# A scheduled attention and MoE kernel: weight signs by ScalarE, scales from squares, one unit fewer in float32

## The chip, the cores and the metric

The kernel runs on one core of a Trainium2 chip. The metric is the device time of one execution in microseconds, less being better. A core has TensorE (PE in the profile; its weight loads are PEld), VectorE (DVE), ScalarE (ACT), GpSimd (POOL), SyncE (SP, which only issues DMAs here) and sixteen DMA engines. Matrix products are written to PSUM, everything else lies in SBUF.

## The reference

```python
# attention with a feature map; q, k, v are (8, 8, 576, 64) float32, w_phi (64, 128)
def phi(x):
    proj = np.einsum('bhsd,df->bhsf', x, w_phi)
    proj = proj - np.max(np.abs(proj), axis=-1, keepdims=True)
    return np.concatenate([np.exp(proj), np.exp(-proj)], axis=-1)
q_p, k_p = phi(q), phi(k)
kv = np.einsum('bhsf,bhsd->bhfd', k_p, v)
z = np.sum(k_p, axis=2)
num = np.einsum('bhsf,bhfd->bhsd', q_p, kv)
den = np.einsum('bhsf,bhf->bhs', q_p, z)[..., None] + 1e-06
attn = (num / den).astype(np.float32)
# then one dense feed-forward; x is (4608, 512), w_in (512, 2048), w_out (2048, 512)
x = attn.transpose(0, 2, 1, 3).reshape(4608, 512)
h = x @ w_in
g = h * (1.0 / (1.0 + np.exp(-1.702 * h)))
out = (g @ w_out).astype(np.float32)
```

`w_in` and `w_out` arrive as float64 and reach the kernel as 64-bit integers.

## The kernel before, in words

**Attention.** The work is cut into 32 units. Unit `i = 4*b + hp` is batch `b` and head pair `hp`: keys and queries of two heads, 512 of the 576 rows. The other 64 rows of all eight heads of a batch (the tail) are handled once a batch by `attn_tail`. A unit can run in two ways. Exact units (`i < NEX`, six of them) work in whole float32: `project_whole` transposes the rows on TensorE and multiplies by `wb`, and each float32 product costs two passes. Split units write each float32 number as a high and a low 16-bit part: `project` makes the two parts on ScalarE and VectorE, turns them by a transposing DMA, and multiplies by `ph`; `features_k` and `features_q` take exponentials, and `parts` forms high parts (`eh`, ScalarE) and low parts (`el`, VectorE's subtraction). The tail always has such parts. In batch 0 its high and low parts are both of the 4-byte type `F32R`, in the other batches the low parts are 16-bit.

**Weights.** There are 32 blocks of 128 x 512 (16 of `w_in`, 16 of `w_out`), prepared in two halves (`NH = 2`). `load_weights` reads a block of float64 into `raw`, views it as a low and a high 32-bit word, and puts a float32 together: POOL scales the high word so that its exponent fits, ScalarE converts the low word, and VectorE merges them, with the sign set last, in two instructions:

```python
R.vector.scalar_tensor_tensor(z, y.bitcast(I32), 3, z, ALU.logical_shift_left, ALU.bitwise_or)
R.vector.scalar_tensor_tensor(
    dst.bitcast(I32), hi, -(2**31), z, ALU.bitwise_and, ALU.bitwise_or)
```

Then four matmuls per block with a one-hot stationary block of nine columns, `pick`, add up the magnitudes by columns in PSUM (`wsum`). `weight_scales` turns those sums into one power-of-two scale for each of the two matrices, and `split_weights` writes each block as a high and a low float16 part, in place.

**MoE.** `moe_chunk` handles 256 or 384 rows at a time over sixteen slices `j` of the hidden width: for each it makes `hb` (three matmuls per 128 of the width: high by high, high by low, low by high), the activation (`th`, `g`), its parts `gh` and `gl`, and three products into each accumulator `ab`. The first 512 rows run half by half, so that they can start when the first half of the weights is ready. The last chunk's three accumulators go to `osb`, `osb` and `e` by ScalarE, and SP stores them, each in two pieces.

**The order of the work.** Nothing is issued as written. Every instruction goes through a `Recorder`, which notes what it reads and writes and its price (`cost`). `R.part(v0, v1)` gives the following instructions virtual times, on a scale where 1 is one MoE chunk of 384 rows and 0 the start of the MoE. `v_att` gives those of the attention units, `V1` those of batch 1, `WV` those of the weights. `schedule` then plays all five engines: each takes, of the instructions whose operands its price list says are ready, the one with the lowest virtual time. Buffers (`NB`, the number of each kind) are handed out in the same play. The result is a fixed order per engine; at run time an engine waits on semaphores for what its next instruction needs and passes nothing by. All instructions therefore bear one line number in the profile, that of the call in `emit`, and are told apart by the names of their tiles.

Of the kernel before, what the change touches and what calls it, by code (L numbers as in the profile page):

```python
# [8 lines left out]
F32 = mybir.dt.float32  # L9
# [3 lines left out]
I32 = mybir.dt.int32  # L13
U32 = mybir.dt.uint32
# [75 lines left out]
class _Op:  # L90
    __slots__ = (
        "eng", "meth", "args", "kw", "cost", "deps", "left", "outs", "allocs", "uses",
        "prio", "load", "passes", "end", "est", "also", "start",
    )


_READY = {"tensor": 282.5, "scalar": 240.0, "vector": 305.0, "gpsimd": 300.0, "sync": 100.0}
# [13 lines left out]
class Recorder:  # L111
# [12 lines left out]

    def tile(self, buf, whole=False):
        tl = _Tile(buf, whole)
        return V(tl, (), buf.aps[0])


    def record(self, eng, meth, args, kw, also):  # L130
        o = _Op()
        o.eng, o.meth, o.args, o.kw = eng, meth, args, kw
# [59 lines left out]
    def cost(eng, meth, args, kw):  # L192
# [9 lines left out]
        if eng == "tensor":  # L202

            wide = mybir.dt.size(ap[1].dtype) == 4
            load = ap[1].shape[-1] / (1.2 if wide else 4.6)
            if meth == "transpose":
# [4 lines left out]
            return (load, n / 2.4 + (14.0 if wide else 3.0), 1)  # L211
# [23 lines left out]


    def schedule(self):
# [16 lines left out]
        pipe, turn, port = 0.0, 0.0, 0.0  # L254
# [20 lines left out]
        while todo:  # L275
            best = None
            for e, c in cand.items():
                t = free[e]
                pick = None
                for o in c:  # L280
                    s = max(t, o.est, turn + o.load) if e == "tensor" else max(t, o.est)
                    ok = True
                    for tl in o.allocs:
                        b = tl.buf
                        if b.ordered and b.head != tl.turn:
                            ok = False
                            break
                        av = [a for a, w in zip(b.avail, b.owner) if w is None]
                        if not av:
                            ok = False  # L290
                            break
                        s = max(s, min(av) + 175.0) if b.head >= len(b.aps) else s
# [26 lines left out]
            elif o.eng == "tensor":  # L319
                turn = s  # L320
# [20 lines left out]
    def emit(self):  # L341
        g = lambda a: a.get() if isinstance(a, V) else a
        self.order = self.schedule()
        for o in self.order:
            f = getattr(getattr(self.nc, o.eng), o.meth)
            f(*[g(a) for a in o.args], **{k: g(a) for k, a in o.kw.items()})  # L346
# [3 lines left out]
def attn_moe_kernel(ctx, tc, q, k, v, w_phi, w_in, w_out, out):  # L350
# [11 lines left out]
    NEX = 6  # L362
# [12 lines left out]
    def static(name, shape, dt):  # L375
# [6 lines left out]
        kq=2, vn=1, xs=2, xT=2, ks=12, tl=1, t=4, e=2, eh=3, el=2, ekth=1, ektl=1,  # L382
        eqth=1, eqtl=1, xf=1, kzs=1, kf=1, lq=2, nf=1, nt=1, xo=1, x=3, th=2, g=2, gh=2,
# [5 lines left out]
        e=([P, 1024], F32), eh=([P, 512], F32R), el=([P, 512], F32R),  # L389
        ekth=([P, 512], F32R), ektl=([P, 512], F32R),  # L390
        eqth=([P, 512], F32R), eqtl=([P, 512], F32R),
# [11 lines left out]
    for nm in ("eh", "el", "ekth", "ektl", "eqth", "eqtl"):  # L403
        pools[nm + "6"] = buf(nm + "6", [P, 512], F16, NB[nm])
    for nm in ("el", "ektl", "eqtl"):
        pools[nm + "b"] = buf(nm + "b", [P, 512], BF16, NB[nm])
# [20 lines left out]
    ones = cp.tile([16, P], F32, name="ones")  # L427
    nc.gpsimd.memset(ones, 1.0)

# [39 lines left out]

    NS = NJ // NH + 1  # L470
    pick = cp.tile([P, 2 * NS - 1], BF16, name="pick")
    nc.gpsimd.memset(pick, 0.0)
    nc.gpsimd.memset(pick[:, NS - 1 : NS], 1.0)

    def load_weights(j, wsum, first, last):
# [4 lines left out]
        for i, src in (  # L480
# [4 lines left out]
            if not WIDE:  # L485
# [3 lines left out]
                z = new("osb")  # L489
                R.scalar.activation(z, wbuf[:, i + 1], AF.Abs)  # L490
            else:
# [3 lines left out]
                else:  # L495
# [165 lines left out]
    pools["kzb"] = buf("kzb", [P, 2, DV], BF16, 1)  # L661
# [12 lines left out]
    for ap in (f32(vs0), v60, f32(vt0), vt60):  # L674
# [6 lines left out]
    for a in range(2):  # L681
        r = slice(a * D, a * D + D)
        for ap in (f32(vt0), vt60):
            nc.gpsimd.memset(ap[r, :, a, 0, D : D + 1], 1.0)

# [121 lines left out]
    def attn_tail(b, tl, exact, bank):  # L807
# [9 lines left out]
        if b == 0:  # L817
            for a in range(2):
# [5 lines left out]
            return ekt, eqt, (vt, vt)  # L824
# [422 lines left out]
```

## Time and profile before

| | |
|---|---|
| median of 3 runs | 1099.08 us (1098.79 to 1100.6) |
| the profiled execution | 1097.82 us |
| its span, first to last instruction | 1096.0 us |
| TensorE busy | 1062.2 us (97%) |
| VectorE busy | 857.8 us (78%) |
| ScalarE busy | 712.2 us (65%) |
| POOL busy | 242.4 us (22%) |
| moved by DMA | 87.80 MB |

How to read the profile's lines. A group line has engine, operation, output and inputs by the program's names (buffer numbers left out), partitions x elements and type, count, busy time in us, the mean duration of one in ns, and the idle time of the engine just before them with what ended it. For matmuls two more sizes stand ahead, rows * columns of the stationary block. A timeline line has start and length in us, then the same, for a run of like instructions (x count), and in brackets the wait before it. A line of stages has the stretch, its length, busy us and count of PE, PEld, DVE, ACT and POOL, the granted clock, the DMA engines' share and GB/s. Matmuls overlap, so that a matmul's duration is longer than what it adds to a run, and busy time of TensorE isn't all work.

### The profile page before, as it was taken

What the parts mean: (1) busy time and instruction counts of PE and PEld (TensorE: products, weight loads), DVE (VectorE), ACT (ScalarE), POOL (GpSimd) and SP (SyncE); (2) the same over time, 40 slices, a digit from 0 to 9 for tenths busy, and PEclk for the clock granted to TensorE, in tenths of its full rate; (3) what the DMA queues carried; (4) which work ended last, traced back from release to release, by engine and by line L of the source; (5) the groups of instructions that cost most, each with busy time, mean ns of one, the idle gap of its engine ahead of it and who ended that gap; (6) DMA issues with size and microseconds to landing.
All of it is one profiled execution on the core that took longest, in us unless ns stands there. A gap on an engine that the chain in (4) does not pass through costs nothing.

```text
span 1096.0 us, 22834 instructions
## 1 busy us (share of the span) xinstructions
PE 1062.2 (97%) x8915; PEld 733.2 (67%) x8915; DVE 857.8 (78%) x1775; ACT 712.2 (65%) x1483; POOL 242.4 (22%) x310
## 2 busy tenths in 40 slices
PE   5997999999999999999999999999999999999997
PEld 3664677778766666678766666677876666577653
DVE  5889988999989997897789987897779877422322
ACT  4576687977677776676777677685677666432423
POOL 6546201322121212221132221121123111100000
PEclk9998999999999999999999999999999999999999
DMA  8854233454243431442243433333223220000101
GB/s 273 277 185 130 76 92 84 79 107 98 61 93 92 96 89 36 81 107 57 32 102 88 109 88 55 64 97 60 49 68 68 39 59 10 11 30 1 30 1 29
DMA packets 174252, 87.80 MB, mean 80 GB/s; under 512 B 140224, under 2 KB 164928, under 8 KB 173888
## 3 DMA queue, kind: packets, MB, share of 16 engines
q1 hardware_dynamic: 174144, 86.34, 33.0%
q8 instruction: 70, 1.15, 0.5%
q14 instruction: 38, 0.31, 0.1%
HBM read 54.59 MB, written 9.44 MB: 58 GB/s over the span
## 4 chain that ended last, share of the span: by engine, by line
PE 78%; DVE 10%; ACT 4%; issue 3%; DMA 2%; POOL 1%; SPq 1%; ACTq 0%; DVEq 0%; POOLq 0%
PE ab L346 31%; PE hb L346 29%; PE at L346 19%; DMA xT<-xs 1%; DVE sm L346 1%; DVE gl L346 1%; ACT e L346 1%; DVE ks L346 1%; DVE g L346 1%; DVE t L346 1%; ACT eh L346 1%; SPq L346 1%; DVE el L346 1%; DVE elb L346 1%; DMA tl<-in_v_dram 1%
## 5 line engine op out<-in xcount | busy, mean ns | idle before, releaser
L346 PE MATMUL hb<-x,wbuf 128*128 128x192 f16 (+3 forms) x3264 | 474.9, 280 | 1.1 <-DVE g L346 1.1
L346 PE MATMUL ab<-wbuf,gh 128*128 128x512 f16 x1152 | 335.8, 380 | 0.8 <-ACT gh L346 0.6
L346 PEld LDWEIGHTS <-wbuf 128*128 128x128 f16 x3264 | 279.1, 98 | 78.0 <-issue 0.9
L346 ACT ACTIVATE th<-hb,usc 128x384 f32<-128x384 f32 (+1 forms) x208 | 116.4, 560 | 130.7 <-PE hb L346 125.0
L346 PE MATMUL ab<-wbuf,gl 128*128 128x512 f16 x576 | 192.2, 380 | 1.3 <-DVE gl L346 1.1
L346 DVE SCALAR_TENSOR_TENSOR g<-th,hb 128x384 f32<-128x384 f32 (+1 forms) x208 | 107.6, 517 | 89.8 <-ACT th L346 87.5
L346 PEld LDWEIGHTS <-gh 128*128 128x128 f16 x1152 | 107.3, 98 | 80.4 <-ACT gh L346 2.9
L346 ACT ACTIVATE gh<-g,al 128x384 f16<-128x384 f32 (+1 forms) x176 | 107.6, 611 | 62.7 <-DVE g L346 62.4
L346 DVE SCALAR_TENSOR_TENSOR gl<-g,al,gh 128x384 f16<-128x384 f32 (+1 forms) x176 | 110.9, 630 | 39.2 <-ACT gh L346 32.9
L346 POOL TENSOR_TENSOR xf<-nf,rc 128x512 f32<-128x512 f32 x28 | 32.8, 1171 | 459.4 <-DVE rc L346 395.1
L346 PE MATMUL at<-ph,xT 128*128 128x128 f16 x944 | 108.6, 221 | 0.4 <-ACT x L346 0.4
L346 ACT ACTIVATE e<-at 128x512 f32<-128x512 f32 x144 | 85.6, 602 | 30.3 <-PE at L346 28.5
L346 DVE TENSOR_REDUCE sm<-at 128x4 f32<-128x512 f32 x126 | 86.1, 683 | 21.3 <-PE at L346 21.1
L346 ACT ACTIVATE e<-t 128x512 f32<-128x512 f32 x144 | 89.9, 640 | 9.8 <-DVE t L346 8.6
L346 PEld LDWEIGHTS <-gl 128*128 128x128 f16 x576 | 55.1, 98 | 51.1 <-DVE gl L346 7.2
L346 DVE SCALAR_TENSOR_TENSOR t<-at,ks,sm 128x512 f32<-128x512 f32 x118 | 87.5, 744 | 1.0
L346 DVE TENSOR_TENSOR el<-e,eh 128x512 f16<-128x512 f32 (+1 forms) x106 | 74.7, 704 | 12.7 <-ACT eh L346 11.1
L346 PE MATMUL at<-vs,eh 128*128 128x132 f32 x208 | 80.2, 386 | 0.0
L346 DVE TENSOR_TENSOR elb<-e,eh 128x512 bf16<-128x512 f32 x104 | 74.8, 719 | 6.7 <-ACT eh L346 6.5
L346 PEld LDWEIGHTS <-xT 128*128 128x128 f16 x944 | 70.2, 98 | 14.3 <-issue 1.3
L346 PE MATMUL at<-kzs,eh 128*128 128x132 f32 x216 | 78.2, 375 | 0.0
L346 ACT ACTIVATE eh<-t 128x512 fp32r<-128x512 f32 x105 | 66.4, 648 | 0.3 <-DVE t L346 0.2
(205 smaller groups left out, 1896.4 us busy)
## 6 DMA issues: line engine op xcount, KB each, us to landing
vn<-in_v_dram SPq DMA_DIRECT2D x64, 128.0 KB, 2.9
kq<-in_k_dram SPq DMA_DIRECT2D x32, 256.0 KB, 3.2
kq<-in_q_dram SPq DMA_DIRECT2D x32, 256.0 KB, 3.0
tl<-in_v_dram SPq DMA_DIRECT2D x18, 384.0 KB, 3.2
x<-in_moe_w_in_dram SPq DMA_DIRECT2D x10, 512.0 KB, 5.3
x<-in_moe_w_out_dram SPq DMA_DIRECT2D x10, 512.0 KB, 4.8
out_dram<-osb SPq DMA_DIRECT2D x38, 128.0 KB, 2.4
out_dram<-osb SPq DMA_DIRECT2D x16, 256.0 KB, 2.5
```

Of the source, the lines that this page charges most:

```text
L346: f(*[g(a) for a in o.args], **{k: g(a) for k, a in o.kw.items()})
```

## The change

1. The sign of a weight is no longer set by VectorE. After the low word's conversion, ScalarE multiplies the high word by a tiny number with a float16 output: what is left is a 16-bit zero that keeps the sign, written into the upper half of the converted low word. One VectorE instruction then merges everything.
2. The scale of a matrix no longer comes from sums of magnitudes. For each 128 columns of a block TensorE multiplies the upper 16 bits (bfloat16) of the finished float32 weights by themselves, so that the diagonal of the 128 x 128 result sums squares; `weight_scales` takes the maximum, transposes, takes it again, halves the exponent by a shift and hands out both scales by one matmul. `pick` is gone.
3. `NEX` is 5 instead of 6: unit 5 becomes a split unit.
4. In batch 0 the low parts are bfloat16, with 16-bit copies of the tail's values (`vtb`) and of `kf` (`kzb`), both written by POOL. In `two`, all `el` kinds now end in `b`.
5. Buffers: `t` 5 instead of 4, `e` 3 instead of 2; the `F32R` low parts are gone.
6. The last chunk: its first accumulator still goes out by ScalarE, the second and third by VectorE, and the second one's stores are issued by ScalarE's queue instead of SP's.
7. The play of the order: a change of stationary size costs TensorE 95 ns, a 4-byte stationary block 22 ns instead of 14, small 16-bit stationary blocks at least 105; several ordered buffers can be taken by one instruction. A new method `pairs` isn't called.
8. Virtual times: as in the diff.

```diff
-    NEX = 6
+    NEX = 5
...
-        kq=2, vn=1, xs=2, xT=2, ks=12, tl=1, t=4, e=2, eh=3, el=2, ekth=1, ektl=1,
-        eqth=1, eqtl=1, xf=1, kzs=1, kf=1, lq=2, nf=1, nt=1, xo=1, x=3, th=2, g=2, gh=2,
+        kq=2, vn=1, xs=2, xT=2, ks=12, tl=1, t=5, e=3, eh=3, ekth=1, eqth=1, xf=1, kzs=1, kf=1, lq=2, nf=1, nt=1, xo=1, x=3, th=2, g=2, gh=2,
...
                 y = wbuf[:, i + 1]
+                R.scalar.activation(lo, lo.bitcast(U32), AF.Copy, scale=0.9375 * 2.0**-29)
                 R.gpsimd.tensor_scalar(y, hi.bitcast(F32), 2.0**-112, None, ALU.mult)
-                z = lo
-                R.scalar.activation(z, lo.bitcast(U32), AF.Copy, scale=0.9375 * 2.0**-29)
+
+                sign = raw.bitcast(F16).rearrange("p (n w) -> p n w", w=4)[:, :, 1]
+                R.scalar.activation(sign, hi.bitcast(F32), AF.Copy, scale=2.0**-60)
                 R.vector.scalar_tensor_tensor(
-                    z, y.bitcast(I32), 3, z, ALU.logical_shift_left, ALU.bitwise_or
+                    y.bitcast(I32), y.bitcast(I32), 3, lo, ALU.logical_shift_left, ALU.bitwise_or
                 )
-                R.vector.scalar_tensor_tensor(
-                    dst.bitcast(I32), hi, -(2**31), z, ALU.bitwise_and, ALU.bitwise_or
-                )
-                z = raw.bitcast(BF16).rearrange("p (n w) -> p n w", w=4)[:, :, 1]
-
-            r = NS - 1 if i % 2 else j % (NS - 1)
+            z = wbuf[:, i + 1].bitcast(BF16).rearrange("p (n w) -> p n w", w=2)[:, :, 1]
             for c in range(NCT):
+                zc = z[:, c * P : (c + 1) * P]
                 R.tensor.matmul(
-                    wsum,
-                    pick[:, NS - 1 - r : 2 * NS - 1 - r],
-                    z[:, c * P : (c + 1) * P],
+                    wsq[:, i % 2],
+                    zc,
+                    zc,
...
-    def weight_scales(k, wsum):
+    def weight_scales(k, wsq):
-        m = small(1, "sc")[0:NS]
-        m2 = small(NS, "sc")[0:NS]
-        R.vector.tensor_reduce(m, wsum, AX.X, ALU.max)
-        pow2(m, m)
-        R.vector.tensor_scalar(m2, ident[0:NS, 0:NS], m, None, ALU.mult)
+        m = small(2, "sc")
+        m1 = small(1, "sc")[0:2]
+        m2 = small(2, "sc")[0:2]
+        R.vector.tensor_reduce(m, wsq, AX.X, ALU.max)
         tp = psa()
-        R.tensor.matmul(tp[:, 0:NS], ones[0:NS], m2, start=True, stop=True)
-        R.vector.tensor_reduce(wg[:, k, 0:1], tp[:, 0 : NS - 1], AX.X, ALU.max)
-        R.vector.tensor_copy(wg[:, k, 1:2], tp[:, NS - 1 : NS])
+        R.tensor.transpose(tp[0:2, 0:P], m, ident)
+        R.vector.tensor_reduce(m1, tp[0:2, 0:P], AX.X, ALU.max)
+        R.vector.tensor_scalar(
+            m1.bitcast(I32), m1.bitcast(I32), 1, 0x7F800000,
+            ALU.logical_shift_right, ALU.bitwise_and,
+        )
+        R.vector.tensor_scalar(m1, m1, 2.0**64, 2.0**-50, ALU.mult, ALU.max)
+        R.vector.tensor_scalar(m2, wone, m1, None, ALU.mult)
+        R.tensor.matmul(tp[:, P : P + 2], ones[0:2], m2, start=True, stop=True)
+        R.vector.tensor_copy(wg[:, k], tp[:, P : P + 2])
...
-        if b:
-            return new(nm + "6"), new(nm + "b" if spare == "el" else nm)
-        return new(spare), new(nm)
+        w = "b" if spare == "el" else ""
+        return new(nm + "6") if b else new(spare + w), new(nm + w)
...
+                R.gpsimd.tensor_copy(vtb[r, :, a, 0:D], tl[r, 2])
-            return ekt, eqt, (vt, vt)
+            return ekt, eqt, (vt, vt, vtb)
...
-            kzl = [z[:, :, 0] for z in kz]
+            kzl = new("kzb")
+            R.gpsimd.tensor_copy(kzl, kf)
+            kzl = [kzl[:, s] for s in range(2)]
...
+            end = c0 + n == SB * S and sb == B // SB - 1
+            osb = new("e")[:, 0:DM] if end and m == n // P - 1 else new("osb")
...
+            elif end and m:
+                R.vector.tensor_scalar(osb, acc[m], osc[:, sb : sb + 1], None, ALU.mult)
+            else:
+                R.scalar.activation(osb, acc[m], AF.Copy, scale=osc[:, sb : sb + 1])
+            store(sb, c0 + m * P, osb, R.scalar if end and m == 1 else R.sync)
...
-    V1 = (-1.1375, 0.5)
-    WV = ((-9.8, 0.3, -7.2), (-7.1, 0.2, -5.4))
+    V1 = (-1.506, 0.476)
+    WV = ((-9.335, 0.3, -7.2), (-7.049, 0.2, -5.399))
+    SV = ((-0.438, 0.02), (0.0, 0.227))
     def v_att(i):
         if i < 4:
-            return -10.175 + i
+            return -10.175 + 0.987 * i
         if i < 8:
             return V1[0] + (i - 4) * V1[1]
-        return 0.825 + (i - 8) * 0.3625
+        return 0.825 + (i - 8) * 0.348
...
-                R.part(u, u + (0.27 if b else 0.1))
+                R.part(u, u + (0.176 if b else 0.1))
...
-            R.part(w, w + (0.54 if b else 0.2))
+            R.part(w, w + (0.537 if b else 0.2))
...
-        R.part(v1, v1 + 0.1, ("vector", "scalar"))
+        v2 = v1 + SV[part_][0]
+        R.part(v2, v2 + SV[part_][1], ("vector", "scalar"))
         for j in js:
             split_weights(j)
```

More of the change, by code (lines that the diff above doesn't have):

```diff
@@ L92 @@
         "eng", "meth", "args", "kw", "cost", "deps", "left", "outs", "allocs", "uses",
-        "prio", "load", "passes", "end", "est", "also", "start",
+        "prio", "load", "passes", "end", "est", "also", "start", "calls",
     )
+_SWITCH = 0.0
 _READY = {"tensor": 282.5, "scalar": 240.0, "vector": 305.0, "gpsimd": 300.0, "sync": 100.0}
@@ L123, in part, with pairs @@
         self.first = first
+    def pairs(self, mm, also=()):
+        o = _Op()
+        o.eng, o.meth, o.args, o.kw, o.calls = "tensor", "matmul", (), {}, mm
+        c = [self.cost("tensor", "matmul", a, k) for a, k in mm]
+        o.load, o.cost, o.passes = c[0][0], _SWITCH + sum(x[1] * x[2] for x in c) / 2, 1
+        o.deps, o.outs, o.allocs, o.uses = {}, [], [], []
+        o.end, o.est = None, 0.0
+        for a, _ in mm:
+            for i in (1, 2):
+                if isinstance(a[i], V):
+                    self.touch(o, a[i], False)
+        for a, _ in mm:
+            self.touch(o, a[0], True)
+        for a in also:
+            self.claim(o, a.tl)
+        o.left = len(o.deps)
+        for d in o.deps:
+            d.outs.append(o)
+        self.group.append(o)
+        o.prio = o.eng in self.first
+        self.ops.append(o)
     def tile(self, buf, whole=False):
@@ L205, in cost @@
             load = ap[1].shape[-1] / (1.2 if wide else 4.6)
+            if ap[1].shape[-1] <= 64 and not wide:
+                return (105.0, max(105.0, n / 2.4), 1)
             if meth == "transpose":
@@ L234, in cost, with mode @@
         return 400.0
+    @staticmethod
+    def mode(o, i):
+        if o.calls:
+            return o.calls
+        st = o.args[1].t if isinstance(o.args[1], V) else o.args[1]
+        n = st.shape[-1] if i else st.shape[0]
+        return 32 if n <= 32 else 64 if n <= 64 else 128
     def schedule(self):
@@ L425, in attn_moe_kernel @@
     nc.vector.tensor_copy(ii[D:P], ident[D:P, D:P])
-    ones = cp.tile([16, P], F32, name="ones")
+    ones = cp.tile([2, P], F32, name="ones")
     nc.gpsimd.memset(ones, 1.0)
+    wone = cp.tile([2, 2], F32, name="wone")
+    nc.vector.tensor_scalar(wone[:, 0:1], ident[0:2, 0:1], 16.0, None, ALU.mult)
+    nc.vector.tensor_copy(wone[:, 1:2], ident[0:2, 1:2])
     wst = static("wst", [P, NF], F32)
@@ L467, in pow2, with load_weights @@
         R.vector.tensor_scalar(dst, dst, 2.0**-50, None, ALU.max)
[L470 to L475, printed above, removed]
+    def load_weights(j, wsq, first, last):
         js = slice(j * P, (j + 1) * P)
@@ L659, in attn_moe_kernel @@
     pools["kz6"] = buf("kz6", [P, 2, 2, DV], F16, 1)
-    pools["kzb"] = buf("kzb", [P, 2, DV], BF16, 1)
+    pools["kzb"] = buf("kzb", [P, 2, 2, DV], BF16, 1)
+    pools["vtb"] = buf("vtb", [P, NHP, 2, DV], BF16, 1)
     pools["v6"] = buf("v6", [P, 8, 2, DV], F16, 1)
@@ L673, in attn_moe_kernel @@
     v60, vt60 = pools["v6"].aps[0], pools["vt6"].aps[0]
-    for ap in (f32(vs0), v60, f32(vt0), vt60):
+    vtb0 = pools["vtb"].aps[0]
+    for ap in (f32(vs0), v60, f32(vt0), vt60, vtb0):
         nc.gpsimd.memset(ap, 0.0)
@@ L817, in attn_tail @@
         if b == 0:
+            vtb = new("vtb")
             for a in range(2):
@@ L926, in attn_unit @@
                 )
-            kzl = [kz[0][:, :, 0], new("kzb")]
+            kzl = [kz[0][:, :, 0], new("kzb")[:, 1]]
             R.gpsimd.tensor_copy(kzl[1], kf[:, 1])
@@ L1064, in out_rows, with store @@
         return b, S - r, r, 1
-    def store(sb, col, osb):
+    def store(sb, col, osb, queue):
         p0 = 0
@@ L1075, in store @@
                 dst = out[row : row + 4 * (n - 1) + 1 : 4, :]
-            R.sync.dma_start(dst, osb[p0 : p0 + n])
+            queue.dma_start(dst, osb[p0 : p0 + n])
             p0 += n
@@ L1120, in moe_chunk @@
                 continue
-            if c0 + n == SB * S and sb == B // SB - 1 and m == n // P - 1:
-                osb = new("e")[:, 0:DM]
-            else:
-                osb = new("osb")
-            if part_ is None:
-                R.scalar.activation(osb, acc[m], AF.Copy, scale=osc[:, sb : sb + 1])
-            else:
+            end = c0 + n == SB * S and sb == B // SB - 1
+            osb = new("e")[:, 0:DM] if end and m == n // P - 1 else new("osb")
+            if part_ is not None:
                 R.vector.scalar_tensor_tensor(
```

57 lines of the change are left out of this document (31 added, 26 removed).

## The prediction

> **What bounds the kernel now.** I read the page's busy shares and slices first, then the busy time by stage, then the instructions around the places where TensorE stands.
>
> ```profile
> span 1096.0 us, 22834 instructions
> PE 1062.2 (97%) x8915; PEld 733.2 (67%) x8915; DVE 857.8 (78%) x1775; ACT 712.2 (65%) x1483; POOL 242.4 (22%) x310
> PE   5997999999999999999999999999999999999997
> DVE  5889988999989997897789987897779877422322
> PEclk9998999999999999999999999999999999999999
> ```
>
> TensorE is busy for 97% of the span. 33.8 us are left, so anything that is to gain more must shorten TensorE's own work. VectorE is next, and only over the first third is it as full as TensorE. By stage (engine columns are busy us; then the granted clock):
>
> ```profile
> 0.00:20.00 20.00, 9.55 (x31) 6.95 (x32) 6.97 (x18) 6.30 (x12) 13.08 (x32) 1.00 0.75 248
> 20.00:120.00 100.00, 88.44 (x547) 60.29 (x546) 91.73 (x167) 69.22 (x137) 53.65 (x36) 0.93 0.67 205
> 140.00:300.00 160.00, 159.20 (x1604) 121.99 (x1602) 151.94 (x343) 122.59 (x278) 36.03 (x51) 1.00 0.40 89
> 300.00:600.00 300.00, 297.03 (x2661) 207.30 (x2659) 262.28 (x540) 215.58 (x450) 66.69 (x89) 1.00 0.36 79
> 600.00:900.00 300.00, 298.31 (x2629) 205.95 (x2628) 253.47 (x530) 207.94 (x440) 64.27 (x91) 1.00 0.33 69
> 900.00:1096.00 196.00, 189.64 (x1328) 117.67 (x1326) 72.87 (x136) 77.03 (x142) 8.67 (x11) 0.99 0.07 17
> ```
>
> There are three regimes. Up to 20 us the first loads land. From 20 to 120 us batch 0's attention and the preparation of the weights share the chip: TensorE stands 11.6 us, VectorE 8.3 us, ScalarE 30.8 us. From 140 to 900 us TensorE stands 5.5 us of 760: there only fewer or shorter matmuls count. The 6.4 us after 900 are the end of the program.
>
> What the 20 to 120 stage waits for:
>
> ```profile
> 101.35 0.68 DVE L346 TENSOR_TENSOR xf<-nf,rc 128x512 f32<-128x512 f32 x1
> 102.08 1.11 PE L346 MATMUL at<-ident,xf 128*128 128x128 f32 x4 [4.07 <-DVE xf L346]
> 112.54 2.05 PE L346 MATMUL hb<-x,wbuf 128*128 128x256 f16 x11
> ```
>
> The last unit of batch 0 waits 4.07 us for VectorE, whose in-order queue has weight instructions ahead of `xf`. After it TensorE runs at reduced clock (mean 0.93 in the stage). The MoE's matmuls are dense only from 112.5 us on. From there TensorE always has work, so each us by which that start comes earlier, and each us of TensorE work removed, should come off the end.
>
> **The change, part by part.** The profiled execution took 1097.82 us (span 1096.0 and 1.8 around it), 1.3 below the median of the three runs shown, 1099.08. I sum against 1097.82 and add 1.3 at the end.
>
> Weight signs.
>
> ```profile
> L346 DVE SCALAR_TENSOR_TENSOR wbuf<-wbuf 128x512 int32<-128x512 int32 x24 | 16.9, 734 | 2.8 <-POOL wbuf L346 2.3 <-issue 0.5
> L346 DVE SCALAR_TENSOR_TENSOR wbuf<-x 128x512 int32<-128x512 int32 x20 | 15.6, 785 | 0.0
> L346 DVE SCALAR_TENSOR_TENSOR x<-wbuf,x 128x512 int32<-128x512 int32 x20 | 14.0, 712 | 0.0
> L346 ACT ACTIVATE x<-x 128x512 int32<-128x512 uint32 x20 | 13.3, 677 | 0.0
> L346 ACT ACTIVATE wbuf<-wbuf 128x512 int32<-128x512 uint32 x12 | 8.1, 695 | 0.0
> ```
>
> Each of 32 blocks has two VectorE instructions, 64 in all, 24 x 0.734 + 20 x 0.785 + 20 x 0.712 = 47.6 us. One of the two goes: 23.8 us off VectorE, nearly all inside 20 to 120, where it falls from 91.7 to about 68. In its place ScalarE gets 32 activations; the nearest are those that convert the low words, 20 x 0.677 + 12 x 0.695 = 21.9 us, so ScalarE rises from 69.2 to 91.1 of 100. The new activation stands between POOL's conversion and VectorE's merge; both wait one ScalarE slot more per block. What is queued behind it on ScalarE is batch 0's exponentials and PSUM copies, and TensorE waits for those.
>
> So the stage passes from VectorE to ScalarE as its fullest engine. If ScalarE keeps the whole 91.1 in it and fills no better than VectorE did (91.7%), the stage lasts 99.3 us: 0.7 gained. But the second half of the blocks isn't needed when the MoE starts, and its two ScalarE passes are 16 x 2 x 0.684 = 21.9 us. If half of that slides behind 120 us, 80.2 / 0.917 = 87 us: 12 gained; by then TensorE's own 88.4 us of work forbid more than about 11. Between 0.7 and 11 I take 7, since TensorE's waits (11.6 us) are what VectorE's relief can remove, and some need ScalarE too.
>
> Scales from squares.
>
> ```profile
> L346 PEld LDWEIGHTS <-pick 128*9 128x9 bf16 x128 | 11.2, 99 | 8.2 <-issue 6.8
> L346 PE MATMUL hb<-wbuf,pick 128*9 128x128 bf16 x32 | 4.6, 290 | 0.0
> L346 PE MATMUL at<-ph,xT 128*128 128x128 f16 x944 | 108.6, 221 | 0.4 <-ACT x L346 0.4
> L346 PE MATMUL at<-ident,t 128*128 128x128 f32 x288 | 48.2, 274 | 0.0
> 70.73 1.55 PE L346 MATMUL hb<-x,pick 128*9 128x128 bf16 x12
> 178.96 1.06 PE L346 MATMUL at<-ph,xT 128*128 128x128 f16 x16
> 132.03 0.60 PE L346 MATMUL at<-ident,t 128*128 128x128 f32 x4
> ```
>
> 128 matmuls stay 128, with a 128-column stationary block instead of 9 columns. In a run of equal matmuls each costs the run less one duration, over count less one. Now: (1.55 - 0.29)/11 = 0.115 us. The nearest rows for the new kind are 16-bit contiguous blocks, (1.06 - 0.22)/15 = 0.056, and float32 ones, which step 4 bytes as the squares do, (0.60 - 0.27)/3 = 0.109. I take 0.109: 0.8 us less, inside the 7 above; 0.056 would give 7.5. The 8.2 us for which weight loads of the 9 columns stood idle may go too, also inside the 7. By the Trainium skill (TensorE: Matmul & The Clock Gate, Weight-path perf modes) the fast weight load is on whenever there are 128 weights of a type other than FP32, strided or not; by that rule the squares would cost like the 0.056 row, and the sum would be 6.7 us lower. No run here shows a strided 16-bit block yet. `weight_scales` becomes a longer chain (a transpose, a second maximum, about 1 us per half): nothing, because batch 0's attention covers the first and running MoE work the second; uncovered, 1 us each.
>
> Five exact units instead of six. Unit 5 (batch 1, head pair 1) leaves the float32 path.
>
> ```profile
> 146.85 3.60 PE L346 MATMUL at<-e,kf 128*66 128x512 f32 x8
> 136.90 1.89 PE L346 MATMUL at<-e,vn 128*66 128x256 f32 x8
> 125.74 1.03 PE L346 MATMUL at<-wb,t 128*128 128x256 f32 x4
> 138.62 0.28 PE L346 MATMUL at<-ekth,vt 128*66 128x128 f16 x2
> 138.98 1.89 PE L346 MATMUL at<-e,vn 128*66 128x256 f32 x8
> 210.95 0.22 PE L346 MATMUL at<-v,eh 128*128 128x132 f16 x1
> 212.09 0.22 PE L346 MATMUL at<-vt,ekth 128*128 128x132 f16 x1
> L346 DVE TENSOR_TENSOR el<-e,eh 128x512 f16<-128x512 f32 x104 | 73.3, 705 | 12.7 <-ACT eh L346 11.1 <-PE at L346 0.8 <-ACT e L346 0.2
> 175.44 1.33 SPq L346 DMA_TRANSPOSE xT<-xs  x1
> ```
>
> Exact, on TensorE: eight matmuls of 256 columns take 138.62 - 136.90 = 1.72 us. The key-value sums are two such runs, 3.4; the projections four runs like the third row, 16 matmuls of the same width, 3.4; the numerators eight of twice the width, 3.4 (the first row's 3.60 has one drain in it); tail terms 2 x 0.36 (138.62 to 138.98), 0.7; six groups of four float32 transposes at 0.109, 2.6; the small rest I estimate at 1.5: 15.0. Split: 32 projection matmuls at 0.056, 1.8; two groups of transposes, 0.9; key-value sums and numerators in groups of four that take (212.09 - 210.95)/3 = 0.38, of which there are 10 and 10, 7.6: together 10.3. The difference, 4.7 us, lies where TensorE is full, so it comes off; I take 4.6. Against it VectorE gains at least eight low parts, 8 x 0.705 = 5.6 us, in a stage where it is 152 of 160 busy; MoE matmuls, which wait for nothing there, cover it. If that cover failed, up to those 5.6 us would show, the upper bound for this step (a loss of 1). SP gains four transposing DMAs of about 1.3 us; later units' loads stand behind them, well ahead of need.
>
> Batch 0's low parts in bfloat16: eight matmuls against `kzs` become 16-bit. A group of four costs 0.38 with a float32 one in it and a 16-bit one costs 0.056, so each can save at most 0.3 us and will save less where its weight load hides: 0 to 2.4, of which I take 0.5. The copies `vtb` and `kzb` lie on POOL, busy 53.7 of 100.
>
> The end.
>
> ```profile
> 1088.83 1.27 ACT L346 ACTIVATE osb<-ab,osc 128x512 f32<-128x512 f32 x2 [1.35 <-PE ab L346]
> 1089.55 2.38 SPq L346 DMA_DIRECT2D out_dram<-osb  x4
> 1089.98 0.69 ACT L346 ACTIVATE e<-ab,osc 128x512 f32<-128x512 f32 x1
> 1092.02 1.19 SPq L346 DMA_DIRECT2D out_dram<-e  x2
> ```
>
> SP issues six stores at 0.6 us each; the last tile is ready at 1090.67 but its stores wait until 1092.02. Two of the six move to ScalarE's queue, so the last two start 1.2 us earlier. Nothing follows: 1.2 gained. ScalarE has issued no DMA so far; were it so slow that its two stores end last, the gain would be 0, and not below.
>
> Buffers, the order's new prices (95 ns for a change of matmul shape) and the virtual times: batch 1's units come before the MoE by up to 1.5 instead of 1.14, and the later units are 4% closer together. They add no instruction. From 300 to 900 us VectorE is 516 of 600 busy; 4% more would be 89%, below the 95% at which TensorE still ran full from 140 to 300. I take 0, within 3 either way.
>
> Sum: 1097.8 - 7 - 4.6 - 0.5 - 1.2 = 1084.5, with 1.3 for the median 1085.8; I say 1085.
>
> **The rivals.** (a) ScalarE simply takes VectorE's place: the stage gains 0.7 and the rest 6.3, 1092. For it: 91.1 of 100; against it: the second half can wait. The rule table of the Trainium skill (ScalarE: Activation LUTs, Rules for kernel authors), which puts multiplication on VectorE, speaks for this one; the rows above, 0.71 to 0.79 us on VectorE against 0.68 to 0.70 on ScalarE, don't bear it out for one instruction. (b) TensorE becomes the only bound up to 120: squares at 0.056 (a further 6.7 us) and the full clock (by the mean of 0.93, 14 us of the stage if that was half speed; I estimate a third of them, 5, as work lost): 1074. The fast-load rule of the Trainium skill, above, speaks for it. (c) Slower: ScalarE keeps waiting between its instructions as it does now (30.8 us idle in the stage), because exponentials and conversions stand in one in-order queue. Then its added 21.9 us are partly serial; half of it, 11, less 6.3, ends near 1104. It decides once dense MoE matmuls start after 112.5 + 6.3 + 2.2 = 121 us. Against it: those waits were mostly for VectorE and TensorE, which have less to do. (d) New stalls of the new order between 140 and 900 us eat up just what is gained: within 2 us of before.
>
> **How the numbers follow.** Forecast 0.54, own range 1078 to 1090; (a) 0.18; (b) 0.13; (c) 0.11; (d) 0.04. What can't be told from no change is 0.2%, 2.2 us. Faster: 0.54 + 0.18 + 0.13 = 0.85, less a little of (a) that ends within: 0.84; same 0.05; slower 0.11. The range takes in (a), most of (b) and stops short of (c): 1071 to 1098.
>
> **What would show it.** VectorE's busy time falls by about 18 us (23.8 less unit 5), ScalarE's rises by over 22. In the 20 to 120 stage VectorE is near 70, ScalarE near 80 to 90; the 4.07 us wait for `xf` and the reduced clock are gone or smaller; dense MoE matmuls start near 105 us. The squares' runs give 0.06 or 0.11 each. There are eight `e,kf` matmuls fewer. From the last matmul to the end 5.2 us instead of 6.4. I am wrong if the MoE starts no earlier, if TensorE's idle time between 140 and 900 us rises above 8 us, or if the squares cost over 0.2 us each.

## The result and the profile after

| | before | after |
|---|---|---|
| median | 1098.93 us (1098.5 to 1100.6, 4 runs) | 1107.18 us (1106.45 to 1107.49, 4 runs) |
| the profiled execution, span | 1097.82, 1096.0 us | 1106.45, 1104.7 us |
| TensorE busy | 1062.2 us | 1053.5 us |
| VectorE busy | 857.8 us | 852.8 us |
| ScalarE busy | 712.2 us | 748.0 us |

The changed kernel takes 1.0076 of the time before, interval 1.0064 to 1.0089. It is 8.3 us slower; the forecast was 1085, with 1098 as the upper end. TensorE does have less to do (8.6 us), but its idle time has grown by 17.3 us. The page of the changed kernel, span, busy shares and slices:

```profile
span 1104.7 us, 22957 instructions
PE 1053.5 (95%) x8943; PEld 724.9 (66%) x8943; DVE 852.8 (77%) x1772; ACT 748.0 (68%) x1520; POOL 242.9 (22%) x320
PE   5887799999999999999999999999999999999997
DVE  5757899999989988997879998987789865322323
ACT  4899888777778666776767676866677665332322
```

A slice is 27.6 us. TensorE's slices two to five have fallen from 9979 to 8877. In the same place VectorE has emptied and ScalarE has filled. By stage:

```profile
20.00:120.00 100.00, 76.13 (x487) 50.70 (x486) 72.54 (x130) 92.69 (x155) 49.68 (x41) 0.94 0.63 196
120.00:140.00 20.00, 18.93 (x138) 12.70 (x136) 17.07 (x37) 17.37 (x32) 4.59 (x3) 0.97 0.22 56
140.00:300.00 160.00, 156.65 (x1623) 119.88 (x1621) 157.87 (x364) 127.86 (x288) 39.47 (x49) 1.00 0.39 87
300.00:600.00 300.00, 296.35 (x2675) 207.16 (x2674) 264.22 (x560) 214.83 (x452) 67.52 (x94) 0.99 0.38 85
600.00:900.00 300.00, 296.82 (x2652) 206.15 (x2650) 261.57 (x535) 210.76 (x445) 61.76 (x91) 1.00 0.32 65
```

From 20 to 120 us VectorE has gone from 91.73 to 72.54, as planned, and ScalarE from 69.22 to 92.69: it is as full as VectorE was. TensorE stands 23.9 us of these 100 instead of 11.6, and 10.2 us instead of 5.5 from 140 to 900 us. The groups that belong to the weights say why ScalarE is so full (last numbers: busy us, mean ns of one):

```profile
L391 ACT ACTIVATE x<-x 128x512 f16<-128x512 f32 x20 | 27.3, 1364 | 0.0
L391 ACT ACTIVATE wbuf<-wbuf 128x512 f16<-128x512 f32 x12 | 16.2, 1374 | 0.0
L391 ACT ACTIVATE x<-x 128x512 int32<-128x512 uint32 x20 | 14.0, 707 | 0.0
L391 ACT ACTIVATE wbuf<-wbuf 128x512 int32<-128x512 uint32 x12 | 8.3, 707 | 0.6 <-DMA wbuf<-in_moe_w_in_dram 0.6
L391 DVE SCALAR_TENSOR_TENSOR wbuf<-wbuf,x 128x512 int32<-128x512 int32 x20 | 14.4, 718 | 8.6 <-issue 4.3 <-ACT x L391 2.1 <-POOL wbuf L391 1.4
L391 PE MATMUL hb<-wbuf 128*128 128x128 bf16 x64 | 5.9, 225 | 0.8 <-DVE wbuf L391 0.8
```

The activation that writes the sign as a 16-bit zero takes 1.36 to 1.37 us, twice the conversion of the low word that the prediction priced it by. The 32 of them take 43.5 us, not 21.9. What TensorE waits for between 20 and 140 us (us in total, times, longest):

```profile
PE at L391 <- ACT xs L391: 3.9, 8, 1.0
PE at L391 <- DVE xf L391: 3.4, 2, 2.6
PE ab L391 <- DVE wbuf L391: 3.2, 4, 1.8
PE ab L391 <- ACT t L391: 3.1, 3, 1.6
PE at L391 <- ACT e L391: 2.3, 1, 2.3
PE at L391 <- ACT kf L391: 2.1, 3, 1.1
```

Most of it is for ScalarE's results of batch 0's attention (11.4 of the 18.1 us shown), which share ScalarE's queue with the weights' instructions. Of single instructions in the timeline:

```profile
38.65 0.86 PE L391 MATMUL hb<-wbuf 128*128 128x128 bf16 x12
...
92.16 0.70 ACT L391 ACTIVATE wbuf<-wbuf,sw 128x512 f16<-128x512 f32 x1
...
110.83 1.10 PE L391 MATMUL at<-ident,xf 128*128 128x128 f32 x4 [2.63 <-DVE xf L391]
...
118.33 3.93 PE L391 MATMUL hb<-x,wbuf 128*128 128x256 f16 x22
...
131.40 0.72 ACT L391 ACTIVATE wbuf<-wbuf,sw 128x512 f16<-128x512 f32 x1
```

The first row is a run of the new squares, told of below. The two rows of ScalarE are the first and the sixteenth split of a weight block, that is, the first half of the weights. The dense MoE matmuls begin at 118.33 instead of 112.54. The wait for `xf` is shorter but still there.

### The profile page after: what moved, and what is told of

Same layout as the page of the kernel before. It is cut to its first block, busy times and chain, and to the rows that moved or that the text cites. A ratio compares the mean times of both kernels' runs of the same rounds, so it can differ in the third digit from the quotient of the medians.

```text
span 1104.7 us, 22957 instructions
## 1 busy us (share of the span) xinstructions
PE 1053.5 (95%) x8943; PEld 724.9 (66%) x8943; DVE 852.8 (77%) x1772; ACT 748.0 (68%) x1520; POOL 242.9 (22%) x320
## 4 chain that ended last, share of the span: by engine, by line
PE 70%; ACT 12%; DVE 10%; DMA 4%; issue 2%; SPq 1%; POOL 1%; DVEq 0%; ACTq 0%; POOLq 0%
PE hb L391 27%; PE ab L391 27%; PE at L391 16%; ACT x L391 3%; ACT e L391 2%; ACT wbuf L391 2%; DMA xT<-xs 2%; DVE sm L391 1%; DVE gl L391 1%; DVE g L391 1%; DVE t L391 1%; ACT xs L391 1%; ACT eh L391 1%; SPq L391 1%; DVE elb L391 1%
## 5 line engine op out<-in xcount | busy, mean ns | idle before, releaser
L391 PEld LDWEIGHTS <-wbuf 128*128 128x128 f16 (+1 forms) x3392 | 285.9, 98 | 87.9 <-DVE wbuf L391 7.1
L391 PE MATMUL ab<-wbuf,gl 128*128 128x512 f16 x576 | 195.2, 381 | 3.1 <-DVE gl L391 3.0
L391 DVE SCALAR_TENSOR_TENSOR t<-at,ks,sm 128x512 f32<-128x512 f32 x122 | 90.8, 745 | 0.9
L391 DVE TENSOR_TENSOR el<-e,eh 128x512 f16<-128x512 f32 x108 | 76.0, 704 | 11.9 <-ACT eh L391 9.1
L391 DVE TENSOR_TENSOR elb<-e,eh 128x512 bf16<-128x512 f32 x110 | 79.6, 723 | 4.7 <-ACT eh L391 3.9
L391 ACT ACTIVATE eh<-t 128x512 fp32r<-128x512 f32 x109 | 68.9, 651 | 2.8 <-DVE t L391 2.7
```

The lines of the kernel that those rows point to most:

```text
L391: f(*[g(a) for a in args], **{k: g(a) for k, a in kw.items()})
```

## Experiments

Each kernel has one edit against another that is named. The planner orders the whole program anew for each, so an edit can also move work far from itself. Ratios are to the kernel before, in the same session. e3, one execution that served for durations alone, isn't in the table.

| kernel | signs by | step of the sign's write | virtual times | median us | ratio, interval |
|---|---|---|---|---|---|
| after | ScalarE | 8 bytes | new | 1107.18 | 1.0076 (1.0064 to 1.0089) |
| e1 | VectorE | – | new | 1093.19 | 0.9946 (0.9932 to 0.9960) |
| e2 | ScalarE, 32-bit | 8 bytes | new | 1091.68 | 0.9935 (0.9922 to 0.9947) |
| e4 | ScalarE, price known | 8 bytes | new | 1104.70 | 1.0049 (1.0037 to 1.0062) |
| e6 | ScalarE | 4 bytes | new | 1094.20 | 0.9955 (0.9942 to 0.9967) |
| e7 | VectorE | – | of before | 1093.39 | 0.9945 (0.9932 to 0.9957) |
| e8 | ScalarE | 4 bytes | of before | 1088.07 | 0.9902 (0.9888 to 0.9916) |
| e9 | as e8, six units | 4 bytes | of before | 1090.65 | 0.9915 (0.9893 to 0.9936) |
| e10 | ScalarE | 8 bytes | of before | 1099.58 | 1.0001 (0.9991 to 1.0012) |
| e12 | as e7, old buffers | – | of before | 1098.76 | 0.9997 (0.9988 to 1.0007) |
| e14 | ScalarE | 8 bytes | weights' new | 1106.60 | 1.0065 (1.0050 to 1.0080) |
| e15 | ScalarE | 8 bytes | units' new | 1101.12 | 1.0016 (1.0006 to 1.0025) |
| e5 | before, five units | – | of before | 1100.06 | 1.0007 (0.9998 to 1.0016) |
| e11 | before, squares | – | of before | 1101.07 | 1.0020 (1.0011 to 1.0030) |
| e13 | before, both | – | of before | 1099.66 | 1.0007 (0.9997 to 1.0016) |

### The sign

**e1: the changed kernel with the sign on VectorE again.**

```diff
-                sign = raw.bitcast(F16).rearrange("p (n w) -> p n w", w=4)[:, :, 1]
-                R.scalar.activation(sign, hi.bitcast(F32), AF.Copy, scale=2.0**-60)
                 R.vector.scalar_tensor_tensor(
-                    y.bitcast(I32), y.bitcast(I32), 3, lo, ...
+                    lo, y.bitcast(I32), 3, lo, ...
+                R.vector.scalar_tensor_tensor(
+                    y.bitcast(I32), hi, -(2**31), lo, ALU.bitwise_and, ALU.bitwise_or
```

> The changed kernel with step 1 alone undone: the sign is set by a second VectorE instruction again, everything else (squares, five exact units, bfloat16 low parts, end, prices, virtual times) as changed. Theory W (a 16-bit output that steps 8 bytes takes ScalarE 1.37 us instead of 0.68, so that the 32 signs cost 43.5 us and ScalarE bounds the stage up to 120 us): ScalarE in 20 to 120 us falls from 92.7 to about 70, TensorE's idle time from 20 to 140 us falls from 24.9 us to 12 or less, the time is 1090 to 1095. Theory O (the new order and virtual times cost the time, whatever engine sets the sign): 1103 or more, with the idle time before 140 us still above 20.

1093.19 us: this one step undone is worth 14 us. The stage of e1:

```profile
20.00:120.00 100.00, 82.25 (x563) 58.03 (x563) 98.93 (x173) 71.57 (x141) 60.86 (x43) 0.93 0.66 204
```

VectorE is full to 98.93 of 100 here, and still TensorE is busy 6 us longer in the stage than in the changed kernel. So with the new virtual times the sign's move costs 14 us. The way there isn't wholly as expected: TensorE's idle time from 20 to 140 us falls from 24.9 to 17.9 us, not to 12, and of the 13.3 us between the two profiled spans 6.0 lie in TensorE's busy time over the whole program, which no run explains.

**e2: the sign by ScalarE as a 32-bit zero over the whole low word.** It leaves out the low three bits of the weights and, by its result and other than its expectation says, their signs.

```diff
-                R.scalar.activation(sign, hi.bitcast(F32), AF.Copy, scale=2.0**-60)
+                R.scalar.activation(lo.bitcast(F32), hi.bitcast(F32), AF.Copy, scale=0.0)
```

> The changed kernel with the same 32 activations on ScalarE, but each writes a 32-bit signed zero over the whole converted low word instead of 16 bits of it; it leaves out the lowest three mantissa bits of the weights. Theory W: the activation takes 0.70 us, ScalarE in 20 to 120 us is 80 to 88, the time is 1085 to 1096. Rival L (ScalarE would be too full even at 0.7 us each, since two activations per block stand in one queue with the exponentials): the stage stays ScalarE's, the time 1101 or more. Theory O: 1103 or more.

1091.68 us. Its 32 activations took 686 and 690 ns:

```profile
L391 ACT ACTIVATE x<-x 128x512 f32<-128x512 f32 x20 | 13.7, 686 | 0.0
```

The instruction stands in the same place of the same chain, so neither the longer chain per block nor a place on ScalarE as such is what costs; the length is.

**e3: five forms of the activation side by side.** Block by block the sign's write takes another form; most signs are left out. `e` has two buffers instead of three here, beside the scratch tiles `sca` and `scb`. One execution was run (1094.71 us), for the durations alone.

```diff
-                R.scalar.activation(sign, hi.bitcast(F32), AF.Copy, scale=2.0**-60)
+                form = i % 8
+                if form in (0, 4): ...   # 16-bit, 8-byte step, as in the change
+                elif form in (1, 5): ... # 32-bit, 8-byte step
+                elif form in (2, 6): ... # 16-bit, contiguous, tile sca
+                elif form == 3: ...      # 16-bit, 4-byte step, tile scb
+                else: ...                # bfloat16, 8-byte step, scale 1.0: values, not zeros
```

> The disputed activation in five forms in one program, by block: float16 stepping 8 bytes (as changed), float32 stepping 8 bytes, float16 contiguous to a scratch tile, float16 stepping 4 bytes to a scratch tile, and bfloat16 stepping 8 bytes with scale 1, so that its values are no zeros. The signs of most blocks are wrong or left out. Theory W: 1.36 for both 16-bit forms stepping 8 bytes, zeros or not; 0.70 for float32; 0.62 to 0.72 for float16 contiguous; the 4-byte step tells whether any step or the wide one costs. Rival Z (results that underflow to zero are slow): 1.36 for all float16 and float32 forms, 0.7 for the bfloat16 one.

The groups of e3, out of one execution:

```profile
L391 ACT ACTIVATE x<-x 128x512 f16<-128x512 f32 x5 | 6.8, 1361 | 0.0
L391 ACT ACTIVATE x<-x 128x512 bf16<-128x512 f32 x4 | 5.4, 1361 | 0.0
L391 ACT ACTIVATE x<-x 128x512 f32<-128x512 f32 x5 | 3.5, 691 | 0.0
L391 ACT ACTIVATE sca<-x 128x512 f16<-128x512 f32 x5 | 3.4, 679 | 0.0
L391 ACT ACTIVATE scb<-wbuf 128x512 f16<-128x512 f32 x3 | 2.4, 794 | 0.0
```

From float32 numbers 8 bytes apart, 512 outputs take 0.68 us as contiguous 16-bit numbers, 0.69 as 32-bit numbers 8 bytes apart, 0.79 as 16-bit numbers 4 bytes apart, and 1.36 as 16-bit numbers 8 bytes apart. Ordinary bfloat16 values cost as much as the zeros. So it is the pair of a 16-bit type and an 8-byte step, and nothing about zeros or tiny results. One thing isn't separated: the 16-bit writes at the 8-byte step all went into the tile that they read, the contiguous ones and those at the 4-byte step into another. Writing into the tile that is read doesn't cost by itself, since the 32-bit numbers do so too at 0.69.

**e4: the changed kernel, with the true price in the planner's list.**

```diff
+        if eng == "scalar" and mybir.dt.size(out.dtype) == 2 and out.ap[-1][0] == 4:
+            return 1320.0
```

> The changed kernel where only the price list knows that a 16-bit ScalarE output stepping 8 bytes takes about 1.37 us, so the fixed order is made for the true length. Theory W (the load itself bounds the stage): ScalarE still has 43.5 us of signs and stays above 90 of 100 in 20 to 120 us; 1102 to 1107. Rival P (the order was made for a wrong price, and that is what stalls): 1098 or less.

1104.70 us: an order that knows the price gets back 2.5 of the 14 us. ScalarE is then busy 95.34 of 100 in the stage. So the wrong price in the planner's list is a small part of the loss; that the order has a larger one, by its virtual times, is shown below.

**e6: the sign still as a 16-bit zero by ScalarE, but 4 bytes apart.** The converted low word goes straight to the weight's own place, the sign into the upper half of each of its words, and POOL's word to where the low word was.

```diff
-                R.scalar.activation(lo, lo.bitcast(U32), AF.Copy, scale=0.9375 * 2.0**-29)
-                R.gpsimd.tensor_scalar(y, hi.bitcast(F32), 2.0**-112, None, ALU.mult)
-                sign = raw.bitcast(F16).rearrange("p (n w) -> p n w", w=4)[:, :, 1]
+                word = y.bitcast(I32)
+                sign = y.bitcast(F16).rearrange("p (n w) -> p n w", w=2)[:, :, 1]
+                R.scalar.activation(word, lo.bitcast(U32), AF.Copy, scale=0.9375 * 2.0**-29)
+                R.gpsimd.tensor_scalar(lo.bitcast(F32), hi.bitcast(F32), 2.0**-112, None, ALU.mult)
```

> The changed kernel with its signs still set by ScalarE as 16-bit zeros, but stepping 4 bytes instead of 8: ScalarE converts the low word into the weight's own place, POOL puts its scaled word where the low word was, and the sign goes into the upper half of the weight's place; the result is the same bit for bit. By the forms the activation then takes 0.79 to 0.82 us, 25.8 in all instead of 43.5. Theory W: ScalarE in 20 to 120 us is below 90, the time near that of the 32-bit zeros, 1090 to 1096. Rival L (two activations per block are too many): 1100 or more.

1094.20 us, 13 less than the changed kernel, with the sign on ScalarE all the same. From e6:

```profile
L391 ACT ACTIVATE wbuf<-x 128x512 f16<-128x512 f32 x20 | 15.9, 797 | 0.0
...
20.00:120.00 100.00, 84.49 (x562) 58.35 (x563) 79.22 (x146) 87.67 (x172) 59.37 (x43) 0.93 0.67 205
```

The activation takes 0.80 us. But e6 is no faster than e1: with the new virtual times, moving the sign at its low price gains nothing.

### The virtual times

**e7, e8 and e10: e1, e6 and the changed kernel with the virtual times of before.** The same edit in all three:

```diff
-    V1 = (-1.506, 0.476)
-    WV = ((-9.335, 0.3, -7.2), (-7.049, 0.2, -5.399))
+    V1 = (-1.1375, 0.5)
+    WV = ((-9.8, 0.3, -7.2), (-7.1, 0.2, -5.4))
-    SV = ((-0.438, 0.02), (0.0, 0.227))
+    SV = ((0.0, 0.1), (0.0, 0.1))
...                       # and the units' pitch and widths
```

> The changed kernel with the sign on VectorE and, beside that, the virtual times of before (V1, WV, v_att, the widths of the parts, the split at v1). Theory T (the new virtual times cause the about 5 us more that TensorE idles between 140 and 900 us): idle there back to about 5.5 us and 1086 to 1090. Rival F (they were chosen for fuller use and help before 140 us): 1095 or more.

> The kernel with 4-byte steps of the signs and the virtual times of before. Theory T: 3 to 6 us below the one with the new times. Rival F: above it.

> The changed kernel as it is (signs as 16-bit zeros at an 8-byte step, 1.36 us each), with the virtual times of before only. If the new virtual times cost the 6.1 us that they cost at the 4-byte step whatever the sign's price: 1100 to 1102.5. If ScalarE's load in 60 to 120 us sets the start of the dense MoE matmuls and the times matter little beside it, as they mattered nothing with the signs on VectorE: 1105 to 1108.

With the sign on VectorE the times change nothing (1093.39 against 1093.19). With it on ScalarE they are worth 6.1 us at the 4-byte step (1088.07 against 1094.20) and 7.6 at the 8-byte step (1099.58 against 1107.18). So e7 alone would have misled: the new times cost only with the sign on ScalarE. At either set of times the shorter write is worth more than that, 13.0 us with the new ones (after, e6) and 11.5 with the old (e10, e8). The first and sixteenth split of e10, beside 92.16 and 131.40 in the changed kernel:

```profile
84.79 0.68 ACT L391 ACTIVATE wbuf<-wbuf,sw 128x512 f16<-128x512 f32 x1
...
122.91 0.70 ACT L391 ACTIVATE wbuf<-wbuf,sw 128x512 f16<-128x512 f32 x1
```

The new times start the first half's loads later (`WV`, -9.335 instead of -9.8). In e10 these splits stand 7.4 and 8.5 us earlier, about as much as the program ends earlier. From e6 to e8 the first split moves from 82.9 to 77.5 and the sixteenth from 119.8 to 112.2; from e1 to e7, where the time stays, from 79.1 to 78.6 and from 116.0 to 116.4. That the later splits are the link between times and end is read from these rows, not tested by itself. They can't be all that sets the end: e7 and e12 (below) have their first splits 2.5 us and their sixteenth 0.3 us apart, and end 5.4 us apart.

**e14 and e15: which times.** e14 is the changed kernel with only the units' times of before, e15 with only the weights' times of before.

```diff
 e14:  V1, and in v_att and attention: pitch 1 and 0.3625, widths 0.27 and 0.54, as before
 e15:  WV and SV as before
```

> The changed kernel with only the virtual times of the attention units as before (their pitch, widths and the start of units 4 to 7); those of the weights' loads and splits are the new ones. If the units' times carry the 7.6 us between the changed kernel and the one with all times of before (the units run up to 12 us ahead of the MoE matmuls from 400 us on): 1099 to 1101.5. If the weights' times carry it: 1105.5 to 1108.

> The counterpart: the changed kernel with only the virtual times of the weights' loads and splits as before, the units' new ones. If the weights' times carry the 7.6 us (their splits 7 us later than in the version with all times of before): 1099 to 1101.5. If the units' times carry it: 1105.5 to 1108. If it is a matter of both together: both of this pair in between.

e14 stays at 1106.60, e15 comes to 1101.12: the weights' times carry some 6 of the 7.6 us, and the units' times by themselves cost little.

### TensorE's savings

**e5: the kernel before with five exact units.**

```diff
-    NEX = 6
+    NEX = 5
```

> The kernel before with step 3 alone: five exact units instead of six, nothing else. The prediction's step says TensorE has 4.6 us less to do and the time falls by about that: 1093 to 1096 against a before of about 1099.5. Rival D (VectorE, with some 6 to 11 us more to do where it is full, holds the MoE back): 1098 or more.

1100.06 us (1.0007, interval 0.9998 to 1.0016), no gain. Of e5, one stage and the sum over all:

```profile
140.00:300.00 160.00, 156.59 (x1614) 118.63 (x1612) 155.27 (x351) 122.36 (x277) 34.59 (x47) 1.00 0.40 87
...
sum 1100.00, PE 1056.10 PEld 727.90 DVE 866.28 ACT 714.86 POOL 247.87; mean PE 150.87 PEld 103.99 DVE 123.75 ACT 102.12 POOL 35.41
```

TensorE's work falls by 6.1 us, more than forecast. VectorE's rises by 8.4, and TensorE, which stood 0.8 us of the 160, now stands 3.4. From 140 to 900 us it stands 10.5 us instead of 5.5. The work that was to cover VectorE's addition doesn't.

**e11: the kernel before with the squares. e13: with the squares and five units.** The edit of e11 is the change's point 2 alone.

```diff
-            r = NS - 1 if i % 2 else j % (NS - 1)
+            z = wbuf[:, i + 1].bitcast(BF16).rearrange("p (n w) -> p n w", w=2)[:, :, 1]
...
-                    wsum, pick[:, NS - 1 - r : 2 * NS - 1 - r], z[:, c * P : (c + 1) * P],
+                    wsq[:, i % 2], zc, zc,
```

> The kernel before with one edit: the scales from squares of the weights' upper halves on TensorE (128 matmuls of 0.058 us for 128 of 0.115), signs still by two operations of VectorE, six units, virtual times of before. Theory S (most of the 5.5 us by which the version with VectorE's signs beats the kernel before is the squares): 1093 to 1095.5, TensorE busy some 7 us less. Rival V (VectorE, busy 92 of 100 us from 20 to 120 us, sets the start of the dense MoE matmuls, and TensorE's saving turns into idle time): 1097.5 to 1099.5.

> The kernel before with both edits that gave nothing alone, the squares and five units in float32; buffers, batch 0's low parts, the end and the virtual times as before. Theory B or any in which the edits left out are needed: 1098 to 1102. If the two need each other (TensorE is freed enough only by both): 1093 to 1096.

1101.07 and 1099.66 us: nothing gained by the squares, nothing by both. e11 is slower than either of its expectations. The stages of e11:

```profile
20.00:120.00 100.00, 82.75 (x556) 57.49 (x554) 96.24 (x167) 70.39 (x138) 50.55 (x36) 0.93 0.66 209
...
140.00:300.00 160.00, 155.10 (x1538) 117.06 (x1537) 146.27 (x331) 121.29 (x274) 34.17 (x48) 1.00 0.36 83
```

TensorE has 6.6 us less to do (1055.5), and the dense MoE matmuls start at 108.3, 4.2 us earlier. But VectorE sits at 96.24 of 100, and the earlier start is given back from 140 to 300 us, where TensorE stands 4.9 us instead of 0.8.

**e12: e7 with the buffers of before.**

```diff
-        ... tl=1, t=5, e=3, eh=3 ...
+        ... tl=1, t=4, e=2, eh=3 ...
```

> The version with the signs on VectorE and the virtual times of before (1093.39 us), with four buffers of t and two of e as before, instead of five and three. Theory B (squares alone and five units alone gave nothing because TensorE waits for t and e; the added buffers are what lets the 5.5 us come out): 1096 to 1099. Rival (the buffers carry nothing, as the prediction took them): 1092 to 1095.

1098.76 against 1093.39 us: the two added buffers carry 5.4 us, about all that e7 gains over before. In e12's timeline, before the MoE:

```profile
110.31 0.40 PE L391 MATMUL at<-ii,zt 128*128 128x64 f16 x4 [3.68 <-ACT zt L391]
...
112.66 1.70 PE L391 MATMUL hb<-x,wbuf 128*128 128x256 f16 x7
```

and in e7's, the same two places:

```profile
105.61 0.39 PE L391 MATMUL at<-ii,zt 128*128 128x64 f16 x4 [1.65 <-ACT zt L391]
...
108.00 1.25 PE L391 MATMUL hb<-x,wbuf 128*128 128x256 f16 x5
```

The MoE starts 4.7 us later with the old buffers. From 20 to 140 us TensorE's waits for ScalarE's `t` are 2.7 us in e12 and 0.3 in e7, those for `zt` 3.7 and 1.7; but its waits for VectorE's `wbuf` before products into `ab` are 4.9 and 8.6. So the runs show what the buffers are worth, and not by which wait. Which of the two does it wasn't tried, and no run has them without the bfloat16 low parts of batch 0.

**e9: e8 with six exact units.**

```diff
-    NEX = 5
+    NEX = 6
```

> The last version (signs as 16-bit zeros at a 4-byte step, virtual times of before: 1088.07 us) with six units in whole float32 again instead of five. Theory D (what TensorE saves on the fifth unit comes back as waits for VectorE and ScalarE's extra splits, as in the kernel before, where it gave 1.1 us more instead of 4.6 less): 1087.0 to 1089.5, and TensorE's idle time from 140 to 900 us some 5 us less than with five. Rival C (with the signs gone from VectorE the splits have room, and the fifth unit pays): TensorE is the limit, its busy time grows by about 6 us, and the time is 1091 to 1094.

1090.65 (0.9893 to 0.9936) against 1088.07 (0.9888 to 0.9916): the intervals overlap, and the run doesn't decide. TensorE's busy time is 1051.4 against 1046.6 us, and its idle time from 140 to 900 us 5.1 against 8.5: most of the saving turns into waits here too.

**The version with the lowest median is e8**: the change with the sign's write at a 4-byte step and the virtual times of before, 1088.07 us, 0.9902 of the time before and 19 us below the changed kernel. Its stage:

```profile
20.00:120.00 100.00, 84.70 (x574) 59.06 (x575) 82.01 (x151) 90.54 (x175) 56.57 (x42) 0.93 0.67 210
```

## Why the prediction was wrong, by its steps

A chain of kernels, from one to the next, gives each step's worth (medians of several sessions; that of the kernel before lay between 1098.9 and 1099.7 in them, so a step is uncertain by about 1 us):

| step | from, to | us | forecast |
|---|---|---|---|
| squares, five units | before 1098.9, e13 1099.7 | +0.8 | -4.6, and the squares in the sign's 7 |
| batch 0's low parts, the end, the planner's prices | e13, e12 1098.8 | -0.9 | -1.7 and 0 |
| buffers | e12, e7 1093.4 | -5.4 | 0 |
| sign by ScalarE, 8-byte step | e7, e10 1099.6 | +6.2 | -7 |
| virtual times | e10, after 1107.2 | +7.6 | 0 |
| sum | | +8.3 | -13.3 |

The last two rows depend on their order, since the new times cost only with the sign on ScalarE: with the times first, they are worth -0.2 (e7 to e1) and the sign's step +14.0 (e1 to after).

**The sign** is the step that failed most. VectorE's relief came (19.2 us in the stage, 23.8 forecast, nearly all of it there). ScalarE's price, 0.677 to 0.695 from the conversions, was wrong: 1.36 measured. The conversions write 32-bit numbers 8 bytes apart, the sign 16-bit ones, and that was taken as the same row. The mechanism wasn't wrong with the virtual times of before: at 0.79 us a piece, e8 against e7, moving the sign gains 5.3 us, near the 7 forecast. With the new times, which the change has, it gains nothing even at that price (e6 against e1, 1.0 us slower). Loss and gain lie on either side of a price that no row of before showed; the prediction gave no upper bound for it. At 43.5 us ScalarE would have come to 69.2 + 43.5 = 112.7 of 100, and the step to a loss.

**Buffers, the order's prices and virtual times**, taken as 0 within 3, failed twice, in opposite directions. The buffers were worth 5.4, the virtual times cost 7.6. That the two add up to 2.2, inside the 3, is luck. The argument on the times looked at the units' pitch from 300 to 900 us; the cost sat in the weights' times, which it passed over.

**Five units**: the forecast of TensorE's work was near (4.7; 6.1 measured), the cover was not. That MoE matmuls cover VectorE's addition stood against a row of VectorE at 151.94 of 160, and the addition was 8.4 us, not 5.6. The upper bound given, a loss of 1, is where e5 lies (1.0 in its session, not told apart from 0).

**Squares**: 0.109 us each was taken, with 0.056 as the other end. The run of twelve took 0.86 us, one alone 0.225: (0.86 - 0.225)/11 = 0.058 each. By that, the trace agrees with the fast weight load in the Trainium skill (TensorE: Matmul & The Clock Gate, Weight-path perf modes), which the prediction didn't follow; e11 shows that the end doesn't hang on it.

**"From there TensorE always has work"**, so that an earlier MoE comes off the end: wrong in e11, where 4.2 us of earlier start came to nothing. The second half's splits weren't earlier there (the first at 136.3, before at 135.6), and VectorE had no room; that this is the reason wasn't tested.

**The end** went by its step. The last rows of the changed kernel:

```profile
1098.77 0.38 PE L391 MATMUL ab<-wbuf,gl 128*128 128x512 f16 x1
...
1099.33 1.19 ACTq L391 DMA_DIRECT2D out_dram<-osb  x2
1100.24 1.50 SPq L391 DMA_DIRECT2D out_dram<-e  x2
```

From the last matmul's end to the end of the span it is 5.5 us, 6.4 before: 0.9 gained, 1.2 forecast.

**The rivals.** (a), ScalarE in VectorE's place, was the right picture at half the price. (b) had the squares right (0.058), but the clock stayed (mean 0.94 in the stage, 0.93 before). (c), the only slower one, gave 1104, near the truth by luck: for another reason (waits between its instructions) and with a condition that wasn't met, dense MoE matmuls at 118.3, not after 121. (d) is there in part: TensorE's idle time from 140 to 900 us grew by 4.7 us. Of the signs named ahead, TensorE's idle time above 8 us from 140 to 900 us (10.2) and an MoE that starts no earlier (118.3) both came and speak against the forecast. VectorE's busy time fell by 5 instead of 18 us: e10 has 17.6 less than e7, but five units add 8.4 and the squares 2.7. That e8's 1088.07 lies in the prediction's own range doesn't bear its sum out: half of that gain is the buffers, which it put at nothing.

## What to carry to other kernels

A row prices an instruction only if type and step of its output agree too; where they don't, put a bound above as well as below, and look whether the step changes its sign between the two. Work taken off a full engine gains only as far as the next ones have room: the 6 us that squares and five units each took off TensorE came to nothing until two more buffers were added. Virtual times tuned for one set of durations are a cost of their own when a duration is different, so try an edit with the old times as well as the new.

## What the runs showed of the hardware

- ScalarE's write of 512 16-bit numbers per partition takes 1.36 us at an 8-byte step, 0.79 at 4 bytes and 0.68 contiguous, while 32-bit numbers at the 8-byte step take 0.69. The Trainium skill (SBUF — State Buffer, the paragraph on cachelines under Door 1: The DMA port swizzle) counts hits per 16-byte line, which are two for both 8-byte writes; these rows differ by a factor of two at the same count, so that rule doesn't give this price. All the 16-bit writes at 8 bytes went into the tile that they read.
- A 128-column stationary block of 16-bit numbers 4 bytes apart costs TensorE 0.058 us per 128 x 128 product, with the moving operand at the same step, about what a contiguous one does (0.056).
